# Pairing the k-v products of two attention units in one visit to the 64x64 tiling

## Chip, cores and metric

The kernel runs on one core of one Trainium2 chip. The metric is the device time of one execution in microseconds (us); lower is better. Single executions of the kernel before took 311.52, 308.06, 313.25 and 309.49 us, a median of 310.5.

## What is computed

Linear attention with softmaxes on q and k, followed by a two-layer block with ELU on all 4608 tokens:

```python
# q, k, v: (8 batches, 8 heads, 576 tokens, 64), float32
q_s = exp(q) / sum(exp(q), over the 64 features)
k_s = exp(k) / sum(exp(k), over the 576 tokens)
kv  = einsum('bhsd,bhse->bhde', k_s, v)
att = einsum('bhsd,bhde->bhse', q_s, kv)
x   = att.transpose(0, 2, 1, 3).reshape(4608, 512)
h   = x @ w_in                                     # (4608, 2048)
g   = where(h > 0, h, exp(min(h, 0)) - 1)
out = g @ w_out                                    # (4608, 512)
```

The maxima that the reference takes off before exp cancel, and the kernel leaves them out.

## The kernel before, in words

**Units.** The attention is cut into 16 units, two for each batch; a unit holds four heads: two on the partition halves f, two in the free dimension h. Its tokens are 9 chunks of 64. Tiles with a buffer number n % 2 are shared by every second unit; there is one raw v buffer `VR` for the units from 4 on, one transposed-q buffer `QT` and, from unit 4 on, one `qsT`.

**A unit's steps.** Loads of q, k and v, 576 KB each, from GpSimd's queue (L321 to L333). `stage1` (L359): exp of q and of k on ScalarE (L365, L368), a cast of v to bf16 `VB` on GpSimd (L373), and for q the sums, reciprocals and scaling on VectorE (L381, L385, L389). From unit 6 on, a DMA transpose of q from SP's queue (`turn`, L425) and a widening cast on GpSimd (`widen`, L433, L435). `kv_mm` (L451): 36 matmuls of 64x64 by 64x65 into columns 384 to 448 of the two banks of one PSUM tile (9 chunks, times 2 f, times 2 h); column 65 of v is ones and gives the sum over k. `m` (L466): a reciprocal and two multiplications on VectorE (L470, L474) make the block matrix `MBLK`. `ao_mm` (L483) in two parts of the chunks, x = 0 and 1 (`part`, L479): two full-array matmuls each, into the same PSUM tile `AB` (number 3), from where ScalarE copies them into the ring `XT` (L513).

**The ELU block.** `hg` (L534): eight 128x512 matmuls into PSUM tile 0 or 1 in turn (L545), exp on ScalarE (L554), then L571 and L573 on VectorE write `GT` (in the first two blocks every second group goes by L565 and L567). `out_mm` (L577, matmuls at L583) and `out_store` (L590, copy L600, stores L609) turn `GT` into output rows. There are nine blocks of 512 tokens with eight groups each.

**Order.** `Sched` is a list scheduler that plans every engine's order beforehand from fixed durations and a model of the loads; a load of a unit from 6 on is taken to land 5000 ns later than that model says (L331). Engines run their planned order in order, with semaphore waits. The main work is a list of `hg` groups; slot s is group s counted from block 0 (eight slots a block). Attention steps are hung on slots (L713 to L720), and an operation hung on a slot is not planned before the start of that slot's group. Unit n has a slot `begin` for stage1 and `use` for its output: units 4 to 7 have (8, 9), (10, 12), (12, 16), (14, 20), and from there (4n - 14, 4n - 8). `ao(n, 0)` stands at use + 1 and `ao(n, 1)` at use + 2; `ao(n, 1)` carries `kv_mm` of unit n + 1 in the same operation on TensorE, and with it the next k load, of unit n + 3, which overwrites the buffer that has just been read. So the k-v products of units 5 to 15 lie at slots 11, 14, 18, 22, 26 and so on to 50, one unit to a visit.

Of the kernel before, what the change touches and what calls it, by code (L numbers as in the profile page):

```python
# [3 lines left out]
AF = mybir.ActivationFunctionType  # L4
# [7 lines left out]
B, H, S, D = 8, 8, 576, 64  # L12
# [4 lines left out]
NU = 2 * B  # L17
CH = 9
BYDMA = 6
# [16 lines left out]
class Sched:  # L36
# [19 lines left out]

    def add(self, eng, dur, emit, key, R=(), W=(), X=(), dma=None, nbytes=0, after=(),
            follow=None, side=0):
        op = Op(eng, dur, emit, key, dma, nbytes)
        op.idx = len(self.ops)  # L60
        op.follow, op.side, op.late, op.gate = follow, side, False, self.gate
        for d in after:
            op.deps[d] = "raw"
        for res in list(R) + list(X):
            for d in self.w.get(res, ()):
                op.deps[d] = "raw"
        for res in list(W) + list(X):
            for d in self.r.get(res, ()):
                op.deps.setdefault(d, "war")
            for d in self.w.get(res, ()):  # L70
                op.deps.setdefault(d, "waw")
        op.deps.pop(op, None)
        for res in R:
            self.r.setdefault(res, []).append(op)
        for res in list(W) + list(X):
            self.w[res] = [op]
            self.r[res] = []
        self.ops.append(op)
        return op
# [164 lines left out]
def t_act(n, psum):  # L244
    return n / 1.2 + (90 if psum else 105)


def t_dve(n, fast=1):
    return n / 0.96 / fast + 75
# [6 lines left out]
class Gen:  # L256
# [49 lines left out]
    def init(self):  # L306
        S = self.S
        S.add("dve", 100, lambda e: e.memset(self.ID[:, :], 0.0), -95, W=["ID"])
        S.add("gp", 300, lambda e: e.affine_select(
            self.ID[:, :], self.ID[:, :], compare_op=ALU.not_equal, fill=1.0, base=0,  # L310
            pattern=[[-1, 128]], channel_multiplier=1), -38, X=["ID"])
        S.add("dve", 60, lambda e: e.memset(self.RZK[0][:, :], 0.0), -90, W=["RZK0"])
        S.add("act", 1400, lambda e: e.activation(self.RZK[0][:, :], self.RZK[0][:, :], AF.Exp), -80,
              X=["RZK0"])
        for i in range(2):
            S.add("dve", 150, lambda e, i=i: e.memset(self.VB[i][:, :, :, D:D + 1], 1.0), -8,
                  W=[f"VBone{i}"])
            S.add("dve", 300, lambda e, i=i: e.memset(self.MBLK[i][:, :, :].bitcast(F32), 0.0), -8,
# [37 lines left out]
        self.gpq = self.S.ops[-1]  # L356
        return self.gpq

    def stage1(self, n, key, vconv="gp"):  # L359
        S = self.S  # L360
        i = n % 2
        q, k, VB = self.RAW[i]["q"], self.RAW[i]["k"], self.VB[i]
        v, vname = self.raw("v", n)
        flat = lambda t: t[:, :, :, :].rearrange("p h c d -> p (h c d)")
        S.add("act", t_act(1152, False), lambda e: e.activation(flat(q), flat(q), AF.Exp),  # L365
              key - 3, X=[f"qR{i}"])
        ek = self.ek(i)
        S.add("act", t_act(1152, False), lambda e: e.activation(  # L368
            ek[:, :, :, :].rearrange("p h c d -> p (h c d)"), flat(k), AF.Exp),
            key - 2, X=[f"kR{i}"])  # L370
        hs = slice(0, 2) if vconv == "gp" else slice(0, 1)
        eng, t = ("gp", 1250) if vconv == "gp" else ("dve", t_dve(576) + 60)
        S.add(eng, t, lambda e: e.tensor_copy(  # L373
            VB[:, hs, :, 0:D], v[:, hs, :, :]), key - 50, R=[vname], W=[f"VB{i}"])
        self.conv = S.ops[-1]
        if vconv != "gp":
            S.add("act", t_act(576, False), lambda e: e.activation(
                VB[:, 1:2, :, 0:D], v[:, 1:2, :, :], AF.Copy), key - 50, R=[vname],
                W=[f"VB{i}x"])
            self.conv2 = S.ops[-1]  # L380
        S.add("dve", t_dve(1152) + 60, lambda e: e.tensor_reduce(  # L381
            self.ZQ[i][:, :, :].rearrange("p h c -> p (h c)"),
            q[:, :, :, :].rearrange("p h c d -> p (h c) d"), AX.X, ALU.add),
            key - 3, R=[f"qR{i}"], W=[f"ZQ{i}"])
        S.add("dve", 250, lambda e: e.reciprocal(self.RZQ[i][:, :, :], self.ZQ[i][:, :, :]),  # L385
              key - 3, R=[f"ZQ{i}"], W=[f"RZQ{i}"])
        rz = self.RZQ[i][:, :, :].unsqueeze(3).broadcast_to([128, 2, CH, D])
        qso = self.QS[self.alt(n)][:, :, :].rearrange("p c (h d) -> p h c d", h=2)
        S.add("dve", t_dve(1152) + 60, lambda e: e.tensor_tensor(  # L389
            qso, q[:, :, :, :], rz, ALU.mult),  # L390
            key - 3, R=[f"qR{i}", f"RZQ{i}"], W=[f"QS{self.alt(n)}"])
# [54 lines left out]
        self.S.add("pe", sum(p[0] for p in parts), mm, key, R=sum((p[1] for p in parts), []),  # L446
                   X=[f"b{2 * ps}", f"b{2 * ps + 1}"], side=1)

    KV = 384

    def kv_mm(self, n, ps):  # L451
        i = n % 2
        P, ek, VB = self.PS[ps], self.ek(i), self.VB[i]

        def mm(e):
            for c in range(CH):
                for f in range(2):
                    for h in range(2):
                        fs, hs = slice(f * 64, f * 64 + 64), slice(h * 64, h * 64 + 64)
                        x = f * 512 + self.KV  # L460
                        last = e.matmul(P[hs, x:x + D + 1], ek[fs, h, c, :],  # L461
                                        VB[fs, h, c, 0:D + 1], start=(c == 0), stop=(c == CH - 1))
            return last
        return CH * 45 + 100, [f"kR{i}", f"VB{i}", f"VB{i}x", f"VBone{i}"], mm

    def m(self, n, ps, key):  # L466
        S, i, rz = self.S, n % 2, self.RZK[n % 2]
        banks = [f"b{2 * ps}", f"b{2 * ps + 1}"]
        PV = self.PS[ps][:, :].rearrange("p (f x) -> p f x", f=2)[:, :, self.KV:self.KV + D + 1]
        S.add("dve", 180, lambda e: e.reciprocal(rz[:, :].unsqueeze(2), PV[:, :, D:D + 1]), key,  # L470
              W=[f"RZK{i}"], X=banks)
        for h in range(2):
            hs = slice(h * 64, h * 64 + 64)
            S.add("dve", 330, lambda e, h=h, hs=hs: e.tensor_tensor(  # L474
                self.MBLK[i][hs, :, h:128:2], PV[hs, :, 0:D],
                rz[hs, :].unsqueeze(2).broadcast_to([64, 2, D]), ALU.mult),
                key, R=[f"RZK{i}"], W=[f"MBLK{i}{h}"], X=banks)

    def part(self, n, x):  # L479
        cut = self.split(n // 2)  # L480
        return (0, cut) if x == 0 else (cut, CH)

    def ao_mm(self, n, x, ps):  # L483
        i = n % 2
# [129 lines left out]
    def program(self):  # L614
        S = self.S
# [10 lines left out]
        AB, C, D_ = 3, 2, 1  # L626
# [38 lines left out]
        def due(n):  # L665

            return when[n][1] + 4 if n in when else 3 + 4 * (n % 2)

        def kv(n):
            def go():  # L670
                self.side(AB, due(n), self.kv_mm(n, AB))
                self.m(n, AB, due(n) - 4)
            return n, go

        def ao(n, x, kvn=None):
            ps, eng = (C if x == 0 else AB, "both") if n == 3 else (AB, "act")

            def go():
                parts = [self.ao_mm(n, x, ps)] + ([self.kv_mm(kvn, ps)] if kvn else [])
                self.side(ps, due(n), *parts)  # L680
                self.xt(n, x, ps, due(n) - 4, eng)
                if kvn:
                    self.m(kvn, ps, due(kvn))
            return n, go

        def first(n):
            def go():
                self.stage1(n, due(n))
                if n >= BYDMA:
                    self.turn(n, due(n))  # L690
            return n, go

        def wide(n):
            if n < BYDMA:
                return n, lambda: self.tp(n, C if n == 3 else AB, due(n) - 4, ("act",))
            return n, lambda: self.widen(n, due(n))

        def loads(*tn):
            def go():
                for t, n in tn:  # L700
                    if n < NU:
                        self.load(n, t, due(n) - 20)
            return 0, go
# [6 lines left out]
        def at(s, *what):  # L710
            slots.setdefault(s, []).extend(what)

        for n in range(4, NU):  # L713
            begin, use = when[n]
            at(begin, first(n), loads(("v", n + 1), ("q", n + 2)))
            at(use - 2 if n >= BYDMA else use, wide(n))
            if n == 4:
                at(use, kv(n), loads(("k", n + 2)))
            at(use + 1, ao(n, 0))
            at(use + 2, ao(n, 1, n + 1 if n + 1 < NU else None), loads(("k", n + 3)))  # L720

        def piece(blocks):
            if steps:
# [9 lines left out]
        key = 0  # L733
# [82 lines left out]
```

## Time and profile before

| | before |
|---|---|
| runs shown | 308.06 to 313.25 us, median 310.5 |
| the profiled execution | 311.22 us, of which 309.4 are the span of the profile |
| PE busy | 296.3 us, 96% of the span, granted clock 0.994 on the mean |
| VectorE, ScalarE, GpSimd busy | 203.4, 162.0, 70.3 us |
| L583 and L545, 128x512 matmuls | 576 each, 144.9 and 144.0 us busy |
| L461, k-v matmuls | 576, 7.8 us busy by the modelled ends |
| L491, attention output matmuls | 64, 14.2 us busy |

A line of the profile's groups or timeline names the source line, engine, operation, the tiles written and read, and the count. Matmuls are pipelined and their ends are modelled; what TensorE really spends is read from the distance between starts. Brackets at the end of a timeline line give idle time ahead of it and what ended it. GpSimd is POOL, VectorE is DVE, ScalarE is ACT.

### The profile page before, as it was taken

To read this page: it belongs to the slowest core of one execution; us is meant where nothing else is said; L and a number is where in the kernel's file an instruction comes from. 1 tells how busy PE (TensorE), PEld (TensorE's weight loads), DVE (VectorE), ACT (ScalarE), POOL (GpSimd) and SP (SyncE) were. 2 spreads that over 40 slices of the span, in tenths; PEclk is the share of its full clock that TensorE was granted. 3 is DMA by queue.
4 is the path that set the end of the run, shared out by engine and by line. 5 is a ranking of instruction groups with operands and counts; after the bars stand their busy time and mean duration, and the time that the engine had idled before them with its cause. 6 is when DMAs were issued, how large, how long until landed. Compare 5 with 4: busy or idle time off the path is not lost.

```text
span 309.4 us, 4597 instructions
## 1 busy us (share of the span) xinstructions
PE 296.3 (96%) x1938; PEld 241.6 (78%) x1938; DVE 203.4 (66%) x244; ACT 162.0 (52%) x190; POOL 70.3 (23%) x84
## 2 busy tenths in 40 slices
PE   7789999989999979999999999999999999999994
PEld 7667787768788868888888888888888888888783
DVE  3837865798998969595969686875544445555500
ACT  4738757979666436464646373734343343333311
POOL 0790144341342435050414130301000000000000
PEclk9979999999999999999999999999999999999999
DMA  7999999797597783938382934131111121111122
GB/s 268 323 365 389 390 390 327 253 294 112 187 284 184 210 239 99 250 81 247 85 243 79 250 80 99 32 74 34 34 36 35 45 48 46 34 34 34 36 68 68
DMA packets 29589, 49.39 MB, mean 160 GB/s; under 512 B 13952, under 2 KB 13952, under 8 KB 29568
## 3 DMA queue, kind: packets, MB, share of 16 engines
q0 software_dynamic: 10336, 33.16, 35.2%
q1 hardware_dynamic: 19232, 15.93, 20.6%
q8 instruction: 15, 0.25, 0.3%
q14 instruction: 6, 0.05, 0.0%
HBM read 36.70 MB, written 9.44 MB: 149 GB/s over the span
## 4 chain that ended last, share of the span: by engine, by line
PE 86%; DVE 5%; DMA 4%; ACT 2%; issue 1%; POOL 1%; SPq 0%
PE PS L583 41%; PE PS L545 40%; DMA VR<-in_v_dram 2%; PE PS L491 2%; DMA W<-in_moe_w_in_dram 2%; DVE ESB L571 1%; PE PS L461 1%; DVE GT L573 1%; ACT ESB L554 1%; DVE QS L389 1%; DVE GT L567 1%; ACT ESB L565 1%; SPq L329 0%; DVE ZQ L381 0%; DVE MBLK L474 0%
## 5 line engine op out<-in xcount | busy, mean ns | idle before, releaser
L545 PE MATMUL PS<-XT,W 128*128 128x512 f32 x576 | 144.0, 394 | 2.8 <-DMA W<-in_moe_w_in_dram 1.2
L583 PE MATMUL PS<-W,GT 128*128 128x512 f32 x576 | 144.9, 393 | 1.7 <-DVE GT L573 1.7
L545 PEld LDWEIGHTS PS<-XT,W 128*128 128x128 f32 x576 | 108.3, 190 | 27.1 <-DVE GT L567 1.8
L583 PEld LDWEIGHTS PS<-W,GT 128*128 128x128 f32 x576 | 106.1, 188 | 24.2 <-DVE GT L573 2.6
L554 ACT ACTIVATE ESB<-PS 128x1024 f32<-128x1024 f32 x72 | 73.9, 1027 | 95.5 <-PE PS L545 95.3
L571 DVE TENSOR_SCALAR ESB<-ESB 128x1024 f32<-128x1024 f32 x64 | 55.5, 867 | 67.4 <-ACT ESB L554 67.1
L573 DVE TENSOR_TENSOR GT<-ESB,PS 128x1024 fp32r<-128x1024 f32 x64 | 78.2, 1221 | 2.2
L600 ACT ACTIVATE OSB<-PS 128x512 f32<-128x512 f32 x32 | 19.2, 600 | 37.0 <-PE PS L583 37.0
L381 DVE TENSOR_REDUCE ZQ<-QR 128x18 f32<-128x1152 f32 x16 | 21.6, 1349 | 6.2 <-ACT QR L365 6.1
L329 POOL DMA_DIRECT2D KR<-in_k_dram x14 | 10.2, 728 | 66.5 <-PE PS L461 66.5
L373 POOL CAST VB<-VR 128x1152 bf16<-128x1152 f32 x15 | 18.3, 1218 | 22.9 <-DMA VR<-in_v_dram 22.9
L389 DVE TENSOR_TENSOR QS<-QR,RZQ 128x1152 f16<-128x1152 f32 x16 | 22.1, 1382 | 0.6
L513 ACT ACTIVATE XT<-PS 128x640 fp32r<-128x640 f32 (+5 forms) x32 | 19.7, 618 | 3.1 <-PE PS L491 3.0
L435 POOL CAST qsT<-QT 128x1152 fp32r<-128x1152 f16 x10 | 13.7, 1372 | 31.0 <-PE PS L461 25.2
L365 ACT ACTIVATE QR<-QR 128x1152 f32<-128x1152 f32 x16 | 18.6, 1165 | 2.8 <-DMA QR<-in_q_dram 2.8
L368 ACT ACTIVATE KR<-KR 128x1152 bf16<-128x1152 f32 x16 | 18.6, 1160 | 1.2 <-DMA KR<-in_k_dram 1.2
L491 PE MATMUL PS<-qsT,MBLK 128*128 128x320 f32 (+3 forms) x64 | 14.2, 306 | 1.1 <-ACT XT L513 0.6
L491 PEld LDWEIGHTS PS<-qsT,MBLK 128*128 128x128 f32 x64 | 11.6, 189 | 4.5 <-DVE MBLK L474 1.0
L329 POOL DMA_DIRECT2D QR<-in_q_dram x14 | 10.3, 738 | 20.0 <-DVE QS L389 20.0
L567 DVE SCALAR_TENSOR_TENSOR GT<-PS,ESB 128x1024 fp32r<-128x1024 f32 x8 | 9.8, 1222 | 6.0 <-ACT ESB L565 6.0
L329 POOL DMA_DIRECT2D VR<-in_v_dram x14 | 10.4, 746 | 3.3 <-POOL VB L373 3.3
L474 DVE TENSOR_TENSOR MBLK<-PS,RZK 64x128 fp32r<-64x128 f32 x32 | 9.3, 289 | 1.1
(28 smaller groups left out, 76.0 us busy)
## 6 DMA issues: line engine op xcount, KB each, us to landing
out_dram<-OSB SPq DMA_DIRECT2D x64, 128.0 KB, 2.4
QR<-in_q_dram POOLq DMA_DIRECT2D x14, 576.0 KB, 5.8
KR<-in_k_dram POOLq DMA_DIRECT2D x14, 576.0 KB, 5.0
VR<-in_v_dram POOLq DMA_DIRECT2D x14, 576.0 KB, 6.4
W<-in_moe_w_in_dram POOLq DMA_DIRECT2D x8, 512.0 KB, 7.8
W<-in_moe_w_out_dram POOLq DMA_DIRECT2D x4, 1024.0 KB, 17.7
QR<-in_q_dram SPq DMA_DIRECT2D x2, 576.0 KB, 4.4
KR<-in_k_dram SPq DMA_DIRECT2D x2, 576.0 KB, 7.0
```

The source lines that it names most:

```text
L329: S.add(eng, ISSUE[eng], lambda e: e.dma_start(dst, src), key, W=[name], dma=f"{name}{eng}", nbytes=128 * 4608, follow=self.gpq if chain e ...
L365: S.add("act", t_act(1152, False), lambda e: e.activation(flat(q), flat(q), AF.Exp), key - 3, X=[f"qR{i}"])
L381: S.add("dve", t_dve(1152) + 60, lambda e: e.tensor_reduce(self.ZQ[i][:, :, :].rearrange("p h c -> p (h c)"), q[:, :, :, :].rearrange("p h ...
L389: S.add("dve", t_dve(1152) + 60, lambda e: e.tensor_tensor(qso, q[:, :, :, :], rz, ALU.mult), key - 3, R=[f"qR{i}", f"RZQ{i}"], W=[f"QS{se ...
L491: last = e.matmul(P[:, f * 512:f * 512 + n_], M[:, f, :], T[:, c0:c1, f * 64:f * 64 + 64], start=True, stop=True)
L513: S.add("act", t_act((h1 - h0) * n_, True), lambda e, dst=dst, src=src: e.activation(dst, src, AF.Copy), key, W=W, X=X)
L545: last = e.matmul(P[:, t * 512:(t + 1) * 512], self.W1[:, kc, tt * 128:(tt + 1) * 128], self.XT[:, kc, rc:rc + BLK], start=(kc == 0), stop ...
L554: S.add("act", t_act(1024, True), lambda e: e.activation(esb[:, :], P[:, :], AF.Exp), key, W=[f"E{i}"], X=banks)
L571: S.add("dve", t_dve(1024, 2) + 80, lambda e: e.tensor_scalar(esb[:, :], esb[:, :], 1.0, -1.0, ALU.min, ALU.add), key, X=[f"E{i}"])
L573: S.add("dve", t_dve(1024) + 90, lambda e: e.tensor_tensor(gt, esb[:, :], P[:, :], ALU.max), key, R=[f"E{i}"], W=gw, X=banks)
L583: last = e.matmul(dst, GT[:, jj, ts * 128:(ts + 1) * 128], self.W2[:, jj, :], start=(jj == 0), stop=(jj == 15))
L600: S.add("act", t_act(512, True), lambda e: e.activation(osb[:, :], src, AF.Copy), key, W=[f"O{i}0", f"O{i}1"], X=[f"b{bk}"])
```

## The change

The k-v products of units 6 and 7, 8 and 9, and so on to 14 and 15 are made in one operation on TensorE, one after the other. The column base moves from 384 to 382, so that two results of 65 columns end at column 512; the second stands at 447. Units 6 and 7 get an operation of their own at slot 16; the other pairs ride with `ao(n, 1)` of the odd unit n ahead of them, at slots 22, 30, 38 and 46. The `m` of both units follow one another.

The k part of `stage1` (exp of k and cast of v) of units 9, 11, 13 and 15 is split off and moves two slots forward, from `begin` of its unit to `begin` + 2 of the unit before; the next v load goes with it. The k loads follow the visits: units 8 and 9 at slot 16 (before: 14 and 18), 10 and 11 at 22 (before: 22 and 26), and so on. `part` now gives x = 1 the shorter part for batch 5 as well (units 10 and 11, cut 3), so that the columns of `ao(11, 1)` and two products fit in a bank. Units 0 to 5 keep their visits.

```diff
-    def stage1(self, n, key, vconv="gp"):
+    def stage1(self, n, key, vconv="gp", what="qk"):
...
+        if "q" in what:
+            S.add("act", t_act(1152, False), lambda e: e.activation(flat(q), flat(q), AF.Exp),
+                  key - 3, X=[f"qR{i}"])
+        if "k" in what:
...
+        if "q" not in what:
+            return
...
-    KV = 384
-
-    def kv_mm(self, n, ps):
+    KV = 382
+
+    def kv_mm(self, n, ps, at=KV):
...
-                        x = f * 512 + self.KV
+                        x = f * 512 + at
...
-        return (0, cut) if x == 0 else (cut, CH)
+        return (0, cut) if x == (cut < 5) else (cut, CH)
...
-                parts = [self.ao_mm(n, x, ps)] + ([self.kv_mm(kvn, ps)] if kvn else [])
+                cols = [(m, self.KV + (D + 1) * y) for y, m in enumerate(kvn)]
+                parts = [self.ao_mm(n, x, ps)] + [self.kv_mm(m, ps, y) for m, y in cols]
                 self.side(ps, due(n), *parts)
                 self.xt(n, x, ps, due(n) - 4, eng)
-                if kvn:
-                    self.m(kvn, ps, due(kvn))
+                for m, y in cols:
+                    self.m(m, ps, due(m), y)
...
+        def kv2(n):
+            def go():
+                cols = [(n, self.KV), (n + 1, self.KV + D + 1)]
+                self.side(AB, due(n), *[self.kv_mm(m, AB, y) for m, y in cols])
+                for m, y in cols:
+                    self.m(m, AB, due(m) - 4, y)
+            return n, go
...
-            at(begin, first(n), loads(("v", n + 1), ("q", n + 2)))
+            late = n > 7 and n % 2
+            at(begin, first(n, "q" if late else "qk"), loads(("q", n + 2)))
+            if not late:
+                at(begin, loads(("v", n + 1)))
+            if n > 6 and n % 2 == 0:
+                at(begin + 2, first(n + 1, "k"), loads(("v", n + 2)))
             at(use - 2 if n >= BYDMA else use, wide(n))
             if n == 4:
-                at(use, kv(n), loads(("k", n + 2)))
+                at(use, kv(n), loads(("k", 6)))
+            if n == 6:
+                at(use, kv2(n), loads(("k", 8), ("k", 9)))
+            pair = n > 6 and n % 2 and n + 1 < NU
             at(use + 1, ao(n, 0))
-            at(use + 2, ao(n, 1, n + 1 if n + 1 < NU else None), loads(("k", n + 3)))
+            at(use + 2, ao(n, 1, (n + 1, n + 2) if pair else (5,) if n == 4 else ()))
+            if n == 4:
+                at(use + 2, loads(("k", 7)))
+            if pair:
+                at(use + 2, loads(("k", n + 3), ("k", n + 4)))
```

More of the change, by code (lines that the diff above doesn't have):

```diff
@@ L364, in stage1 @@
         flat = lambda t: t[:, :, :, :].rearrange("p h c d -> p (h c d)")
[L365 to L380, printed above, removed]
+        if "q" in what:
+            S.add("act", t_act(1152, False), lambda e: e.activation(flat(q), flat(q), AF.Exp),
+                  key - 3, X=[f"qR{i}"])
+        if "k" in what:
+            ek = self.ek(i)
+            S.add("act", t_act(1152, False), lambda e: e.activation(
+                ek[:, :, :, :].rearrange("p h c d -> p (h c d)"), flat(k), AF.Exp),
+                key - 2, X=[f"kR{i}"])
+            hs = slice(0, 2) if vconv == "gp" else slice(0, 1)
+            eng, t = ("gp", 1250) if vconv == "gp" else ("dve", t_dve(576) + 60)
+            S.add(eng, t, lambda e: e.tensor_copy(
+                VB[:, hs, :, 0:D], v[:, hs, :, :]), key - 50, R=[vname], W=[f"VB{i}"])
+            self.conv = S.ops[-1]
+            if vconv != "gp":
+                S.add("act", t_act(576, False), lambda e: e.activation(
+                    VB[:, 1:2, :, 0:D], v[:, 1:2, :, :], AF.Copy), key - 50, R=[vname],
+                    W=[f"VB{i}x"])
+                self.conv2 = S.ops[-1]
+        if "q" not in what:
+            return
         S.add("dve", t_dve(1152) + 60, lambda e: e.tensor_reduce(
@@ L464, in kv_mm, with m @@
         return CH * 45 + 100, [f"kR{i}", f"VB{i}", f"VB{i}x", f"VBone{i}"], mm
-    def m(self, n, ps, key):
+    def m(self, n, ps, key, at=KV):
         S, i, rz = self.S, n % 2, self.RZK[n % 2]
         banks = [f"b{2 * ps}", f"b{2 * ps + 1}"]
-        PV = self.PS[ps][:, :].rearrange("p (f x) -> p f x", f=2)[:, :, self.KV:self.KV + D + 1]
+        PV = self.PS[ps][:, :].rearrange("p (f x) -> p f x", f=2)[:, :, at:at + D + 1]
         S.add("dve", 180, lambda e: e.reciprocal(rz[:, :].unsqueeze(2), PV[:, :, D:D + 1]), key,
@@ L673, in kv, with ao, first @@
             return n, go
-        def ao(n, x, kvn=None):
+        def ao(n, x, kvn=()):
             ps, eng = (C if x == 0 else AB, "both") if n == 3 else (AB, "act")
             def go():
-                parts = [self.ao_mm(n, x, ps)] + ([self.kv_mm(kvn, ps)] if kvn else [])
+                cols = [(m, self.KV + (D + 1) * y) for y, m in enumerate(kvn)]
+                parts = [self.ao_mm(n, x, ps)] + [self.kv_mm(m, ps, y) for m, y in cols]
                 self.side(ps, due(n), *parts)
                 self.xt(n, x, ps, due(n) - 4, eng)
-                if kvn:
-                    self.m(kvn, ps, due(kvn))
+                for m, y in cols:
+                    self.m(m, ps, due(m), y)
             return n, go
-        def first(n):
+        def kv2(n):
             def go():
-                self.stage1(n, due(n))
-                if n >= BYDMA:
+                cols = [(n, self.KV), (n + 1, self.KV + D + 1)]
[3 more added lines that the diff above has]
+            return n, go
+        def first(n, what="qk"):
+            def go():
+                self.stage1(n, due(n), what=what)
+                if n >= BYDMA and "q" in what:
                     self.turn(n, due(n))
```

## The prediction

> **What bounds the kernel now.** I read the shares of busy time, then the chain that ended last, then the windows by stage, then TensorE's own timeline around two slots that differ only in a k-v product. The first two say that TensorE sets the end.
>
> ```profile
> PE 296.3 (96%) x1938; PEld 241.6 (78%) x1938; DVE 203.4 (66%) x244; ACT 162.0 (52%) x190; POOL 70.3 (23%) x84
> ...
> PE 86%; DVE 5%; DMA 4%; ACT 2%; issue 1%; POOL 1%; SPq 0%
> ```
>
> The windows show where it does not: PE's busy time is below the length of the stretch from 60 to 112 us and full from 112 to 290. In the same early stretch DVE is busy for about nine tenths.
>
> ```profile
> 60.00:78.00 18.00, 16.61 (x147) 13.12 (x148) 16.35 (x24) 15.71 (x18) 6.53 (x8) 1.00 0.81 202
> 78.00:92.00 14.00, 13.70 (x95) 10.97 (x94) 12.92 (x15) 9.73 (x12) 5.88 (x7) 1.00 0.75 221
> 92.00:112.00 20.00, 18.35 (x116) 14.82 (x116) 18.00 (x20) 9.52 (x11) 8.89 (x10) 1.00 0.74 197
> ...
> 128.00:216.00 88.00, 88.00 (x597) 72.43 (x596) 66.03 (x76) 46.45 (x56) 20.97 (x20) 1.00 0.47 125
> ```
>
> So from 112 us on a nanosecond that leaves TensorE's queue leaves the time; ahead of that, orders matter as much as work. Third, TensorE alone, over a slot without a k-v product (unit 8's part 0) and one with (part 1 and unit 9's product):
>
> ```profile
> 114.47 0.46 PE L491 MATMUL PS<-qsT,MBLK 128*128 128x320 f32 x2
> 114.77 1.99 PE L583 MATMUL PS<-W,GT 128*128 128x512 f32 x8
> 116.60 1.98 PE L545 MATMUL PS<-XT,W 128*128 128x512 f32 x8
> 118.42 0.40 PE L491 MATMUL PS<-qsT,MBLK 128*128 128x256 f32 x2
> 118.75 0.49 PE L461 MATMUL PS<-VB,KR 64*64 64x65 bf16 x36
> 119.17 2.12 PE L583 MATMUL PS<-W,GT 128*128 128x512 f32 x8
> 121.12 0.40 PE L545 MATMUL PS<-XT,W 128*128 128x512 f32 x1
> ```
>
> Starts count: 116.60 - 114.47 = 2.13 us without, 121.12 - 118.42 = 2.70 with. The second has 2 x 64 columns less of attention output; eight 512-column matmuls take 116.60 to 118.42 = 1.82, so 128 columns are 0.06. One visit therefore costs 2.70 - 2.07 = **0.63 us**. Of that the 36 matmuls themselves are the smaller half: their row is 0.49 long, one of them 0.19 (their median), so 36 starts lie within 0.30. The other **0.33** is the visit: about 0.09 before the first start (0.33 from 118.42 to 118.75, against 0.24 for 512 columns at the full rate), 0.12 after the last (119.05 to 119.17), and 0.13 that the L583 group behind it takes longer (1.95 to the next start, against 1.82).
>
> **The change, part by part, against the profiled execution (span 309.4, time 311.22, 0.7 above the median of 310.5).**
>
> *Visits.* Units 6 to 15 have ten visits now and five afterwards; units 0 to 5 are untouched. The matmuls stay. Five times 0.33 is **-1.65**. Ends: if a second product costs its whole distance from first start to the next group (119.17 - 118.75 = 0.42), five times 0.21 is -1.05; if only the pace of the last starts counted (12 starts in 0.09, so 0.27 for 36) it is -1.8. I take 1.65, since the second product finds the array in its tiling already. The Trainium skill, page TensorEngine Tiling (Array Packing), section Instruction Overhead, speaks against this: about 60 cycles for each matmul, one column as slow as 60. At the pace of the L583 row (512 columns in 0.2275 us) 60 are 0.027, and 36 such 0.96 us as an estimate, more than a whole visit here: by it five pairings would cost 5 x (0.96 - 0.63) = +1.65. The row has 36 starts in 0.30 us, 8 ns each, and the row decides.
>
> *Own operation for units 6 and 7, part order of batch 5, columns 382 and 447.* The visit is counted above. The same matmuls and copies run in another order for units 10 and 11: zero, covered by the ring, whose chunks are due in slot 40 while the short part now comes in slot 38 (two slots of 3.6 us against one L513 copy of about 0.5). Odd columns are read by L470 and L474, 0.16 and 0.31 a piece, on an engine off the path: zero either way, with no row for it; even doubled, 0.77 a unit is under the DVE slack worked out below.
>
> *m of two units at once.* No instruction more, but 0.16 + 0.61 = 0.77 of DVE work of the odd unit comes four slots earlier, behind the even one's. Look at the DVE behind the visit at 118.75:
>
> ```profile
> 120.56 1.64 DVE L571 TENSOR_SCALAR ESB<-ESB 128x1024 f32<-128x1024 f32 x1
> 122.23 1.22 DVE L573 TENSOR_TENSOR GT<-ESB,PS 128x1024 fp32r<-128x1024 f32 x1
> 123.37 0.16 DVE L470 RECIPROCAL RZK<-PS 128x2 f32<-128x2 f32 x1
> 123.56 0.61 DVE L474 TENSOR_TENSOR MBLK<-PS,RZK 64x128 fp32r<-64x128 f32 x2
> ```
>
> L573 ends at 123.45 and frees the PSUM tile that the group at 124.76 writes: 1.31 of slack. 0.77 fits, and the alternate slots have no visit, so DVE gets back. Zero; at the other end, if the two k loads that now stand in POOL's queue ahead of the widening push L571 by another 0.72, 0.77 + 0.72 - 1.31 = 0.18 over, at four pairs +0.7.
>
> *POOL's queue.* The k loads (0.72 of issue each) go out in twos; casts and v loads of odd units from 9 on pass the widening of the even unit. POOL is busy 23% and its time is mostly waiting for k-v products; in the steady part a k load is issued some 13 us ahead of its exp (119.55 and 132.97), so that two at once still land in time. SP's queue (transposes, stores) keeps its order, zero. Where it can hurt is the stall that is there already:
>
> ```profile
> 102.02 3.40 DVE L571 TENSOR_SCALAR ESB<-ESB 128x1024 f32<-128x1024 f32 x1 [0.43 <-ACT ESB L554]
> ...
> 110.71 2.11 PE L583 MATMUL PS<-W,GT 128*128 128x512 f32 x8 [1.65 <-DVE GT L573]
> ```
>
> L571 usually takes 0.69. At 102.02 it waits out POOL's widening (102.62) and cast of v9 (103.71, ends 104.87), and ends 0.55 after the cast; DVE is late from there, and PE stands 1.65 at 110.71. The page SBUF — State Buffer, section Who interferes with whom, has the rule: one exclusive lock for VectorE's fast modes and GpSimd. By that rule a queued load's issue would hold it too, as a sentence by itself: two loads, 1.4. No row shows that: L571 at 108.72 took 0.69 beside the load issued at 109.09. Afterwards the cast of v9 stands before the visit, which takes 1.16 off that wait, and m of unit 9 puts 0.77 on. I take **0** net for the stall, ends -1.65 (gone) and +0.8.
>
> *New wait.* A visit now waits for exp of k and cast of v of both units, and `ao(7, 1)` waits with it; behind it on PE stand the groups. Cast v7 ended at 80.66 + 1.15 = 81.81, and PE could be at the slot 16 visit at 79.54: up to 2.4 with a hop. Cast v9 ended at 104.87, and PE was at `ao(7, 1)` at 100.77: up to 4.2. I take 0, since the planner puts the visit behind its own idea of these casts, and that adds 5 us to each load; TensorE then has other groups to run, and a later visit costs nothing until slot 25, where `ao(8, 0)` needs it.
>
> Sum: -1.65 + 0 + 0 = 309.6 for the profiled execution, and 310.5 - 1.65 = **308.9** as a median, its own range 308.7 to 310.2 by the ends of the visits and of DVE.
>
> **Rivals.**
> *The stall at 110.71 goes.* For: the cast that made it leaves its place. Against: two k loads and a second m take that place. 308.9 - 1.65 = 307.2.
> *PE waits for the younger unit's v* (the slower side). Place: visits 6/7 and 8/9; price 2.4 and 4.2 as above; it turns the gain into a loss from 1.65 of waiting on. For: v7 and v9 pass through one buffer, each load starting only after the cast before it (v9's load was issued at 93.50, landing about 6.4 later, cast 1.16: 101.1, just when PE is there). Against: the planner's 5 us. At 8/9 alone 308.9 + 4.2 = 313.1, at both 315.5.
> *No gain:* the 0.33 is a price of each product and not of the switch. For: nothing shows two products in a row before. Against: 36 starts in 0.30 us. 310.5.
>
> **How the numbers follow.** Forecast 0.53, stall gone 0.17, wait for v 0.22 (0.09 at one pair, 0.13 at both), no gain 0.08. About 1% (3.1 us) is what a measurement of this kernel can tell from no change. Faster by more: 0.12 of the second case, which lies right at that bound, and 0.03 of the first: 0.15. Slower by more: the wait at both pairs, 0.13. The rest, 0.72, is within. The range, 306.6 to 313.2, reaches from just under the stall's going to the wait at one pair; it leaves out the wait at both and a little below. I expect 308.9.
>
> **What would show it.** Eleven groups of starts at L461 in place of sixteen, five of them with 72 matmuls in about 0.6 us; each pair's slots 0.33 shorter in sum than before from 112 us on. A forecast gone wrong shows as idle PE ahead of L491 or L461 with POOL L373 as its end near 80 or 101 (wait for v), ahead of L583 or L545 with DVE L573 (stall kept or grown), or as a second product longer than 0.42.

## The result, and the profile after

The changed kernel takes 308.84 us as a median of 54 runs, against 310.18 of 78 runs of the kernel before: a ratio of 0.9961, 95% interval 0.9948 to 0.9975, or 0.8 to 1.6 us less. The profiled execution took 308.63 us, with a span of 306.8 (before: 311.22 and 309.4). Two further measurements gave 0.9943 (0.9917 to 0.9969) and 1.0008 (0.9972 to 1.0043): the second, alone, shows no difference. Medians are of all executions of a kernel, ratios of those within 1.5% of its fastest.

In the changed kernel the lines stand up to four further down: its L465, L495, L549, L587, L575 and L577 are L461, L491, L545, L583, L571 and L573 of the kernel before, and its L571 is L567. The page of the changed kernel: the same 1938 matmuls, and in the chain that ended last TensorE is still the largest share, though 72% instead of 86: the chain now runs back through a load of v that lands near 44 us, to the start-up.

```profile
PE 293.7 (96%) x1938; PEld 239.6 (78%) x1938; DVE 199.2 (65%) x244; ACT 162.4 (53%) x190; POOL 72.5 (24%) x84
...
PE 72%; DMA 10%; DVE 8%; POOL 5%; ACT 3%; issue 1%; SPq 0%; DVEq 0%
```

The same stretches in its windows (length, PE busy, PEld, DVE, ACT, POOL, granted clock, DMA share, GB/s): from 92 to 112 us PE is busy for 19.70 of 20 instead of 18.35, from 78 to 92 it has lost 0.45.

```profile
60.00:78.00 18.00, 16.60 (x115) 13.13 (x114) 16.01 (x20) 15.69 (x19) 5.83 (x8) 1.00 0.71 214
78.00:92.00 14.00, 13.25 (x127) 10.50 (x126) 12.65 (x17) 7.83 (x9) 6.62 (x8) 1.00 0.69 199
92.00:112.00 20.00, 19.70 (x158) 16.00 (x157) 15.18 (x19) 11.43 (x14) 8.82 (x9) 1.00 0.73 199
...
128.00:216.00 88.00, 87.92 (x600) 72.53 (x599) 63.64 (x77) 46.26 (x55) 20.68 (x20) 1.00 0.45 122
```

TensorE's timeline at the pair of units 10 and 11:

```profile
132.17 0.40 PE L495 MATMUL PS<-qsT,MBLK 128*128 128x256 f32 x2
132.50 0.78 PE L465 MATMUL PS<-VB,KR 64*64 64x65 bf16 x72
133.21 2.11 PE L587 MATMUL PS<-W,GT 128*128 128x512 f32 x8
135.15 1.98 PE L549 MATMUL PS<-XT,W 128*128 128x512 f32 x8
```

72 starts take 133.21 - 132.50 = 0.71 us to the next group, where 36 took 0.42: the second product costs 0.29. The edges are unchanged: 0.33 from L495 to the first product, and the group behind takes 1.94 instead of 1.82. And two places at which PE idles, with what ended it:

```profile
80.19 2.11 PE L549 MATMUL PS<-XT,W 128*128 128x512 f32 x8 [0.75 <-DVE GT L571]
...
109.33 2.12 PE L587 MATMUL PS<-W,GT 128*128 128x512 f32 x8 [0.30 <-DVE GT L577]
```

The first was 0.30 before, the second 1.65.

To add this up I take the distance from each matmul's start to the next, less its rate (227 ns for 512 columns), from the first matmul of slot 12 (65 us) to the last. "Edges" is what lies at the two ends of the visits and in the first matmul behind; "stalls" is every other excess of over 130 ns, without stretches of half clock. Start-up, which differs between executions, is outside.

| us | slot 12 to the last matmul | edges | stalls |
|---|---|---|---|
| before, two profiles | 239.44, 239.27 | 3.24, 3.24 | 2.27, 2.07 |
| changed, three profiles | 237.46, 237.40, 237.44 | 1.63, 1.63, 1.63 | 1.61, 1.60, 1.61 |

The visits take 1.61 us less. The stalls are another matter: before 0.46 at slot 17 and 1.82 (1.61) near 110; changed 0.91 at slot 17, 0.47 near 109 and 0.24 near 203. The rest, what the table leaves of the distance, is 0.2 to 0.3 more in the changed kernel, about as much as the smallest of these stalls; its cause is open.

### The profile page after: what moved, and what is told of

It is laid out like the page before. It is cut to its first block, busy times and chain, and to the rows that moved or that the text cites. A ratio compares the mean times of both kernels' runs of the same rounds, so it can differ in the third digit from the quotient of the medians.

```text
span 306.8 us, 4600 instructions
## 1 busy us (share of the span) xinstructions
PE 293.7 (96%) x1938; PEld 239.6 (78%) x1938; DVE 199.2 (65%) x244; ACT 162.4 (53%) x190; POOL 72.5 (24%) x84
## 4 chain that ended last, share of the span: by engine, by line
PE 72%; DMA 10%; DVE 8%; POOL 5%; ACT 3%; issue 1%; SPq 0%; DVEq 0%
PE PS L587 36%; PE PS L549 33%; DMA VR<-in_v_dram 10%; DVE GT L577 2%; PE PS L495 2%; POOL W L345 2%; DVE ESB L575 2%; DVE QS L393 1%; ACT ESB L558 1%; DVE ZQ L385 1%; POOL VB L375 1%; PE PS L465 1%; DVE GT L571 1%; POOL W L354 1%; ACT ESB L569 1%
## 5 line engine op out<-in xcount | busy, mean ns | idle before, releaser
L549 PE MATMUL PS<-XT,W 128*128 128x512 f32 x576 | 142.7, 392 | 3.4 <-DMA W<-in_moe_w_in_dram 1.4
L587 PE MATMUL PS<-W,GT 128*128 128x512 f32 x576 | 144.4, 392 | 0.4 <-DVE GT L577 0.3
L549 PEld LDWEIGHTS PS<-XT,W 128*128 128x128 f32 x576 | 106.9, 188 | 27.6 <-DVE GT L571 2.4
L587 PEld LDWEIGHTS PS<-W,GT 128*128 128x128 f32 x576 | 106.2, 188 | 22.9 <-DVE GT L577 1.8
L575 DVE TENSOR_SCALAR ESB<-ESB 128x1024 f32<-128x1024 f32 x64 | 49.6, 775 | 67.6 <-ACT ESB L558 67.2
L577 DVE TENSOR_TENSOR GT<-ESB,PS 128x1024 fp32r<-128x1024 f32 x64 | 78.2, 1221 | 2.2
L375 POOL CAST VB<-VR 128x1152 bf16<-128x1152 f32 x15 | 21.5, 1436 | 26.0 <-DMA VR<-in_v_dram 26.0
L439 POOL CAST qsT<-QT 128x1152 fp32r<-128x1152 f16 x10 | 12.4, 1243 | 56.0 <-PE PS L495 38.9
L393 DVE TENSOR_TENSOR QS<-QR,RZQ 128x1152 f16<-128x1152 f32 x16 | 23.4, 1464 | 0.5
L495 PE MATMUL PS<-qsT,MBLK 128*128 128x320 f32 (+3 forms) x64 | 14.2, 306 | 1.1 <-ACT XT L517 0.6
L495 PEld LDWEIGHTS PS<-qsT,MBLK 128*128 128x128 f32 x64 | 11.6, 189 | 4.5 <-ACT XT L517 1.0
L571 DVE SCALAR_TENSOR_TENSOR GT<-PS,ESB 128x1024 fp32r<-128x1024 f32 x8 | 9.8, 1224 | 6.4 <-ACT ESB L569 6.3
```

What stands on the lines that cost most here:

```text
L375: S.add(eng, t, lambda e: e.tensor_copy(VB[:, hs, :, 0:D], v[:, hs, :, :]), key - 50, R=[vname], W=[f"VB{i}"])
L393: S.add("dve", t_dve(1152) + 60, lambda e: e.tensor_tensor(qso, q[:, :, :, :], rz, ALU.mult), key - 3, R=[f"qR{i}", f"RZQ{i}"], W=[f"QS{se ...
L495: last = e.matmul(P[:, f * 512:f * 512 + n_], M[:, f, :], T[:, c0:c1, f * 64:f * 64 + 64], start=True, stop=True)
L549: last = e.matmul(P[:, t * 512:(t + 1) * 512], self.W1[:, kc, tt * 128:(tt + 1) * 128], self.XT[:, kc, rc:rc + BLK], start=(kc == 0), stop ...
L575: S.add("dve", t_dve(1024, 2) + 80, lambda e: e.tensor_scalar(esb[:, :], esb[:, :], 1.0, -1.0, ALU.min, ALU.add), key, X=[f"E{i}"])
L577: S.add("dve", t_dve(1024) + 90, lambda e: e.tensor_tensor(gt, esb[:, :], P[:, :], ALU.max), key, R=[f"E{i}"], W=gw, X=banks)
```

## The experiments

My theory was that each visit costs 0.32 us beside its matmuls and that this makes the gain. The rival was that the moved loads and casts make it, by way of the stall near 110. Each run has its ratio to the kernel before, with the interval.

**The changed kernel again.** 

> The changed kernel again, as the measure for the next ones on the same chip. Both theories expect about 1.2 to 1.8 us under the kernel before. What differs in the profile from the first one of the changed kernel shows which idle times of TensorE are fixed by the order and which come and go with the landing of loads.

Measured: 308.63, ratio 0.9943 (0.9917 to 0.9969). From slot 3 to the end no slot's first matmul differs from the first profile by more than 0.1 us once the start is aligned (-0.27 at slot 8, -0.31 at the end), so its three stalls belong to the order.

**Pairs split in two visits.**

```diff
-                parts = [self.ao_mm(n, x, ps)] + [self.kv_mm(m, ps, y) for m, y in cols]
+                kvs = [self.kv_mm(m, ps, y) for m, y in cols]
+                parts = kvs[:1] + [self.ao_mm(n, x, ps)] + kvs[1:] if len(kvs) > 1 else (
+                    [self.ao_mm(n, x, ps)] + kvs)
```

> The four pairs from unit 8 on keep their operation, slot and everything else, but the attention output's two matmuls stand between the two products, so that TensorE enters the 64x64 tiling twice. Theory (each visit costs about 0.32 us beside its matmuls): about 4 x 0.32 = 1.3 us slower than the changed kernel, that is near the kernel before, and from slot 27 on the distance to the changed kernel grows by about 0.3 at each of slots 30, 38 and 46. Rival (the gain is the stall near 110 us that got shorter when loads and casts moved): equal to the changed kernel within 0.3 us.

Measured: 309.19, ratio 0.9982 (0.9950 to 1.0014), on the chip on which the changed kernel had 0.9943. Its timeline has two visits around the output's matmuls:

```profile
133.37 0.48 PE L465 MATMUL PS<-VB,KR 64*64 64x65 bf16 x36
133.79 0.50 PE L495 MATMUL PS<-qsT,MBLK 128*128 128x256 f32 x2
134.22 0.48 PE L465 MATMUL PS<-VB,KR 64*64 64x65 bf16 x36
134.63 2.11 PE L587 MATMUL PS<-W,GT 128*128 128x512 f32 x8
```

Against the changed kernel slots 24, 31, 39 and 47 are each 0.30 to 0.32 later: the price, four times, 1.26 in the edges (2.89 against 1.63). But at slots 25 and 49 it takes 0.33 and 0.32 back: the waits for GT near 109 and 203 shrink, since TensorE comes to them later. Net 0.6 us by the profile. The medians are 0.56 apart (309.19 and 308.63), the ratios 0.0039, which is 1.2 us, and their intervals overlap. So the theory's price is right, the rival is wrong that nothing would change, and two of the four savings only lengthen a wait for VectorE.

The same run says how the gain is shared. From slot 12 on the split kernel needs 239.48 us, and 1.4 of that is a stretch of half clock at 65.6 us (last section) that the others don't have there. Without it, it is 1.2 to 1.3 us under the kernel before and 0.65 to 0.7 over the changed one. By the profiles, then, four pairs bring a third of the gain, and the new order around them, by way of the stall near 110, about two thirds. By the ratios (0.9982 and 0.9943) it is the other way round: two thirds for the pairs. The shares stay open between these two.

**The moves without the pairs.** From unit 9 on the k parts and v loads as in the changed kernel, every product alone:

```diff
...
-            if n == 6:
-                at(use, kv2(n), loads(("k", 8), ("k", 9)))
-            pair = n > 6 and n % 2 and n + 1 < NU
...
-            at(use + 2, ao(n, 1, (n + 1, n + 2) if pair else (5,) if n == 4 else ()))
-            if n == 4:
-                at(use + 2, loads(("k", 7)))
-            if pair:
-                at(use + 2, loads(("k", n + 3), ("k", n + 4)))
+            at(use + 2, ao(n, 1, (n + 1,) if n + 1 < NU else ()), loads(("k", n + 3)))
```

> Exp of k, cast of v and the next v load of units 9, 11, 13 and 15 two slots earlier and the part order of batch 5 as in the changed kernel, but every k-v product in a visit of its own, in the slots of the kernel before. Theory (the visits make the gain): within 0.5 us of the kernel before, apart from what the stall near 110 us does. Rival (the moved casts make it, by taking the 1.65 us stall away): 1.2 to 1.7 us under the kernel before, with no idle time of over 0.5 us ahead of L587 near 110 us.

Measured: 312.21, ratio 0.9991 (0.9945 to 1.0037); 241.14 us from slot 12 on, with edges of 3.28, stalls of 2.57 and 1.6 at half clock (last section). The stall near 110 is not gone but 2.1. VectorE and TensorE there:

```profile
101.58 3.37 DVE L575 TENSOR_SCALAR ESB<-ESB 128x1024 f32<-128x1024 f32 x1
...
110.53 3.17 PE L587 MATMUL PS<-W,GT 128*128 128x512 f32 x8 [1.95 <-DVE GT L577]
```

The planner left the cast of v9 behind the widening on GpSimd, and L575 waited out both, as before. In this execution, of 312.49 us, the earlier slots alone did not remove the stall, against the rival. The times don't settle it: three of the twelve took 307.8 to 308.0, the other nine 311.3 to 314.6, and none of the three was profiled. They may have been without the stall, and the interval reaches down to the rival's 1.2 to 1.7 us.

**Pairs from unit 8 on.** Units 6 and 7 as before, at slots 14 and 18:

```diff
-            if n == 6:
-                at(use, kv2(n), loads(("k", 8), ("k", 9)))
...
-            at(use + 2, ao(n, 1, (n + 1, n + 2) if pair else (5,) if n == 4 else ()))
-            if n == 4:
-                at(use + 2, loads(("k", 7)))
+            at(use + 2, ao(n, 1, (n + 1, n + 2) if pair else (n + 1,) if n < 7 else ()))
+            if n < 7:
+                at(use + 2, loads(("k", n + 3)))
```

> Units 6 and 7 keep single visits, at slots 14 and 18 with the k loads of the kernel before; pairs from unit 8 on. If a visit is worth its 0.32 us wherever it is, this is 0.3 us slower than the changed kernel. If the visit at slot 14 was hidden, because TensorE waits for VectorE's GT at slot 17 anyway (0.46 us there before, 0.91 in the changed kernel), then it is 0.3 us faster than the changed kernel, since only the visit of unit 7 is left in the full part, 0.62 instead of 0.91.

Measured: 309.39, ratio 0.9967 (0.9921 to 1.0013), but the profile needs 236.52 us from slot 12 on, 0.94 less than the changed kernel, with edges of 1.98 and stalls of 0.68. One more visit, 0.35 of edges, and ahead of slot 17:

```profile
81.52 0.72 PE L549 MATMUL PS<-XT,W 128*128 128x512 f32 x2 [0.30 <-DVE GT L571]
```

0.30 as in the kernel before, not 0.75. The visit of unit 6 at slot 14 was hidden: taken out, TensorE comes to the same wait 0.45 earlier, and the product is paid at slot 18, where nothing hides it. The stall near 109 is absent in this profile too (0.47 in the changed kernel), and counts for as much. The times don't confirm the better order, so I ran it once more.

> Pairs from unit 8 on, once more, beside the changed kernel on the same chip. Its first profile had 0.94 us less TensorE time from slot 12 on than the changed kernel, yet its times were spread from 307.1 to 312.4. If the order is better as such, its median is 0.5 to 1 us under the changed kernel. If the spread belongs to the order (an idle time that comes in some executions only), about two in five of its times are over 311 us again and the median is not under the changed kernel's.

Measured: 308.17, ratio 0.9953 (0.9917 to 0.9988), 1.1 us under the changed kernel beside it (309.3). But its profile needs 238.55 us from slot 12 on, two more than its first: L393, which overwrites the tile that the transpose of q reads, waited 2.9 us for that transfer, and VectorE's delay reached TensorE ahead of L587 (1.22) and, at 115.59, ahead of the output's matmuls (0.47).

```profile
106.11 1.36 DVE L393 TENSOR_TENSOR QS<-QR,RZQ 128x1152 f16<-128x1152 f32 x1 [2.91 <-DMA QT<-QS]
...
108.10 1.22 DVE L577 TENSOR_TENSOR GT<-ESB,PS 128x1024 fp32r<-128x1024 f32 x1
109.24 3.46 DVE L575 TENSOR_SCALAR ESB<-ESB 128x1024 f32<-128x1024 f32 x1
...
109.38 2.11 PE L587 MATMUL PS<-W,GT 128*128 128x512 f32 x8 [1.22 <-DVE GT L577]
```

The order can win 0.9 and doesn't always. As a faster version it stays unclear: 0.8 us over the changed kernel on one chip, 1.1 under it on the other.

> The changed kernel, beside the other two of this call: 308.2 to 309, 1.2 to 1.8 us under the kernel before, idle times ahead of slot 17 and near 109 and 203 us as in both of its profiles (0.9, 0.5, 0.2).

Measured: 309.3, ratio 1.0008 (0.9972 to 1.0043); stalls of 0.91, 0.47 and 0.24 again. On this chip the changed kernel was not the faster one, though its profile is the same to 0.06 us.

**Eight visits at each pair, and the same work in one.** Full-array matmuls of 32 columns, spread or in front; every round starts its own sum (`True` is `False` in the second kernel):

```diff
...
+            for _ in range(1 if True else 8):
+                other()
...
+                    if True and left[0] and k and k % 2 == 0:
+                        other()
```

> The changed kernel, with eight full-array matmuls of 32 columns added at each of the five pairs: one ahead of the products, seven spread between their rounds, so that TensorE enters the 64x64 tiling eight times at each pair instead of once. To allow that, every round writes over the one before: the sum over the chunks is left out, in this kernel and in the next alike; order and work of the other engines are those of the changed kernel. Theory (0.32 us for each entry and exit, beside the matmuls): 35 more visits than the next kernel, so 35 x 0.32 = 11 us slower than it, less some 1 us of waits that the longer visits take the place of. The part of the 0.32 that lies in the following 512-column group (0.1) may shrink with 32 columns behind it: no less than 35 x 0.2 = 7 us. Rival (a price of the product, not of the entry): within 1 us of the next kernel.

> The same 72 product matmuls and eight matmuls of 32 columns at each pair as in the kernel before this one, with all eight ahead of the products: one visit at each pair. Both theories: 40 small matmuls are 40 x 0.02 to 0.06 = 0.8 to 2.4 us more TensorE time than the changed kernel.

Measured: 316.1 and 309.37, ratios 1.0196 (1.0156 to 1.0237) and 0.9980 (0.9948 to 1.0012): 6.7 us between them. Edges 9.47 and 1.59, so 7.88 for 35 visits, 0.225 each. That still holds the small matmul between two visits, which takes 0.03 where eight stand in a row; the whole distance from slot 12 on grew by 7.04 (238.00 to 245.04), 0.20 each. The second kernel needs 0.5 more than the changed one, with stalls that are 0.45 shorter (1.16), so 1.0 for its small matmuls. At one pair of the first kernel:

```profile
107.73 0.19 PE L817 MATMUL PS<-ID 128*128 128x32 f16 x1
107.85 0.26 PE L833 MATMUL PS<-VB,KR 64*64 64x65 bf16 x8
108.03 0.19 PE L817 MATMUL PS<-ID 128*128 128x32 f16 x1
108.15 0.26 PE L833 MATMUL PS<-VB,KR 64*64 64x65 bf16 x8
```

From product to product 0.30 us, of which two rounds are 0.065 by the 0.29 for nine. In and out is a price of the visit and not of the product. It is the lower end that I gave, 0.2: what is missing against 0.32 is about the 0.1 in the following 512-column group, which has no place behind 32 columns.

**The stall near 110 by itself.** In the kernel before, the widening of unit 8 is planned a slot later:

```diff
-            at(use - 2 if n >= BYDMA else use, wide(n))
+            at(use - 1 if n == 8 else use - 2 if n >= BYDMA else use, wide(n))
```

> The kernel before, single visits, with one step moved: the widening cast of unit 8 on GpSimd one slot later, so that it no longer stands between the k load at 101.9 and the cast of v9. Theory on the stall: TensorE's 1.65 us near 110 come from L571 waiting out widening and cast on GpSimd (3.40 instead of 0.69); with one of the two gone L571 ends 1.16 earlier and the stall is 0.5 or less, as in the changed kernel: 1.2 us under the kernel before, about equal to the changed one, with all sixteen visits. Rival (the visits make the whole difference between the kernels): equal to the kernel before within 0.4 us.

Measured: 310.8, ratio 1.0009 (0.9983 to 1.0035), with a profile at a clock of 0.85 throughout, which can't be laid beside the others.

> The kernel before with the widening cast of unit 8 one slot later, again, because its first profile ran at a clock of 0.85 throughout and can't be laid beside the others. Theory on the stall: L571 near 102 us takes 2.3 instead of 3.4, and TensorE's idle time near 110 is 0.5 to 0.7 instead of 1.65. Rival (the stall has another cause, the backlog on VectorE as a whole): over 1.2 as before.

Measured: 310.56, ratio 1.0032 (0.9999 to 1.0065). In the profile:

```profile
101.34 2.31 DVE L571 TENSOR_SCALAR ESB<-ESB 128x1024 f32<-128x1024 f32 x1 [0.43 <-ACT ESB L554]
```

2.31 as worked out, TensorE idles 0.6 ahead of L583, the stall is 0.72 instead of 1.82, and 238.40 us are needed from slot 12 on, 1.0 less than before. So GpSimd's chain made that stall in that execution. The times do not show the 1.0. The reason may be that the kernel before has this stall in other forms:

> The kernel before, profiled a second time. Its times lie in two groups, 308.0 to 309 and 310 to 312. If the stall near 110 us is fixed by the order, this profile has it again: L571 of 3.4 us near 102 and 1.6 to 2 us of idle time ahead of L583, and the groups come from elsewhere (the clock, the start). If the stall comes and goes with who is first at GpSimd's and VectorE's contested step, a profile of the lower group has L571 at 0.7 to 2.3 and less than 0.8 of idle time, with the rest of the order unchanged.

Measured: 309.74, ratio 0.9988 (0.9939 to 1.0037). The second profile of the kernel before has a stall of 1.61, with L571 at 0.69:

```profile
100.86 0.69 DVE L571 TENSOR_SCALAR ESB<-ESB 128x1024 f32<-128x1024 f32 x1 [0.43 <-ACT ESB L554]
...
105.11 1.36 DVE L389 TENSOR_TENSOR QS<-QR,RZQ 128x1152 f16<-128x1152 f32 x1 [1.58 <-DMA QT<-QS]
106.38 1.64 DVE L571 TENSOR_SCALAR ESB<-ESB 128x1024 f32<-128x1024 f32 x1
```

Neither outcome that I had written down: the stall is there, with another cause, the transpose of q, for which L389 waited. What is the same is the place: VectorE comes late out of 100 to 110 us, and the output's matmuls at slot 25 start only when it has written the GT group just ahead of them (L573 until 110.65 and L583 at 110.71 in the first profile).

**m first.** Pairs from 8, with `self.m(m, ps, due(m) - 8, y)`; the `m` of the single units 5 to 7 go ahead with it.

> Pairs from unit 8 on, as tried before, and the three VectorE steps of a pair's units with a key 8 smaller, so that the planner takes them ahead of the ELU steps. It is meant as a faster version: the idle time ahead of L587 near 203 us (0.22) came where both units' steps stood ahead of L575. Expected 0.9 us less TensorE time from slot 12 on than the changed kernel, as pairs from 8 gave, and 0.2 for the stall near 203; against it, that they now delay an earlier L575 by up to 1.5 us, which the 1.3 us of slack there need not cover: then a stall of up to 0.3 at each of the four pairs.

Measured: 309.83, ratio 0.9999 (0.9976 to 1.0021). The stall near 203 is gone, but two new ones of 1.05 came, at the pairs at 131 and 163 us, and 238.59 us are needed from slot 12 on, 1.1 more than in the changed kernel; VectorE and TensorE at the first:

```profile
134.69 2.52 DVE L575 TENSOR_SCALAR ESB<-ESB 128x1024 f32<-128x1024 f32 x1
...
138.53 0.73 PE L549 MATMUL PS<-XT,W 128*128 128x512 f32 x2 [0.90 <-DVE GT L577]
```

Both units' steps ahead of L575 take 1.66 (133.00 to 134.66), and push it under GpSimd's widening and cast. That is more than the 1.3 us of slack.

## Why the prediction held, and where its steps were off

*Visits, -1.65.* Right as the price: -1.61 in the edges, 0.29 for the second product where I had 0.30, 0.20 to 0.225 a visit without the following group, 0.32 with it. The eleven groups of starts, five of them with 72 matmuls, came as forecast.

*All five counted.* This step failed. I had read that TensorE waits before 112 us, and still priced the pair of units 6 and 7 like the rest. Its saving at slot 14 went into the wait at slot 17 (0.46 to 0.91). Units 6 and 7 in single visits gave that back, at 0.35 of edges. Nor does every nanosecond count from 112 us on, as I had it: by the split pairs, the savings at units 8 and 9 and at 14 and 15 went into the waits near 109 and 203 us (0.33 and 0.32). Of the five savings two reached the end in these profiles.

*m of two units, 0 with an end of +0.7.* 0.24 near 203, at one pair of four; splitting the pairs took it away, and so did the m steps at other times. Where they went ahead of L575, the slack of 1.3 that I had worked out was the limit, as the two stalls of 1.05 show.

*The stall near 110, 0 with ends of -1.65 and +0.8.* Mis-sized: 1.82 and 1.61 in the two profiles of before, 0.47 in all three of the changed kernel, so -1.1 to -1.4. I had expected two k loads to take the place of the cast. But L575 at 107.33 started with the first load's issue and took 0.69, and the second m came behind the ELU step.

```profile
107.33 1.55 POOL L329 DMA_DIRECT2D KR<-in_k_dram  x2 [8.59 <-PE PS L465]
107.33 0.69 DVE L575 TENSOR_SCALAR ESB<-ESB 128x1024 f32<-128x1024 f32 x1
```

*Wait for v, the slower rival.* It did not come: in the changed kernel's waits TensorE stands 0.7 us in all for L375's VB at L465, near 11 and 46 us, both ahead of the first pair. The five pairs did not wait for v.

*The sum.* By the first profiles -1.61 - 1.35 + 0.45 + 0.24 = -2.3, and -2.0 with the small rest; by the ratio -1.2. That the point forecast of -1.65 stood between these is luck: terms that I had set to nothing have opposite signs, and the largest of them, the stall, outweighs what the pairs bring net by the profiles. What makes the times gain less than the profiles is open. Single times of the kernel before reach down to 307.87, near the fastest of the changed one beside it, 307.73, so the stall near 110 may be absent in some of its executions; neither of its two profiles shows that. The half clock of the last section may have a part. The profiled executions of the changed kernel had a mean granted clock of 0.998 or 0.999. Its 17 executions at 0.996 or more have a median of 308.20, against 310.20 for 20 such executions of the kernel before in the later measurements: 2.0, as in the profiles. At 0.990 to 0.995 it is 309.07 (33) against 310.07 (72), 1.0. The 20 reach from 307.8 to 311.8 and come from three chips, so this is a hint and not shown.

## What to carry to other kernels

A change of tiling is paid per visit, so products that need it belong together; the price is read from the distance between starts across a visit and across its neighbour without one. A saving is worth its size only where the engine that saves has nothing to wait for behind it: look for the next wait on that engine, and count the saving only as far as that wait doesn't take it. Where the order comes from a planner, moving one step changes which operations meet on other engines, and such meetings can outweigh the step itself.

## What the runs showed of the hardware

TensorE's clock was halved for one stretch of 3.4 us after idle time. In the profile of the moves without the pairs, TensorE idled 1.95 us ahead of 110.53; the windows (PEclk is the third number from the right) then show 0.50:

```profile
107.00:111.20 4.20, 2.25 (x11) 1.55 (x10) 4.13 (x5) 1.02 (x1) 1.99 (x3) 1.00 0.70 190
111.30:114.70 3.40, 3.40 (x9) 2.67 (x8) 1.27 (x2) 0.60 (x1) 0.50 (x1) 0.50 0.88 279
114.70:118.00 3.30, 3.30 (x16) 2.73 (x15) 0.82 (x2) 1.91 (x3) 0.00 (x0) 1.00 0.46 137
```

Nine matmuls started in 3.4 us where 15 have room at 227 ns: 1.6 us lost behind a stall of 2.1. The kernel before idled 1.65 at the same place and lost nothing there; its own half-speed stretch lay at 16.7 to 20.1 us. The splitting of the pairs had one at 65.6, behind idle times of 0.55 and 0.85. So a stall can cost nearly twice its length in one execution and not in the next. One stretch of 3.4 us at half speed takes 0.0055 off the mean clock of a 307 us span, so the mean tells how many an execution had: of the 54 executions of the changed kernel, 17 at 0.997 or more have a median of 308.20 us, 33 at 0.992 to 0.994 one of 309.07, four at 0.983 one of 313.07.

VectorE's L575 against GpSimd: started at 107.33, with a load's issue, it took 0.69. Started within one (109.24, with a load's issue until 109.91), it waited for that, for the widening and for the cast (end 112.15) and took 3.46. The Trainium skill, page SBUF — State Buffer, section Who interferes with whom, says that of VectorE in a two-port mode and GpSimd the one that issues first has the shared ports for its whole instruction. Both rows agree with that. Close behind a load's start it came out both ways. In the first profile of the kernel before, L571 started 0.12 us behind one and took 3.40; in the second it started 0.13 behind and took 0.69, and there the load's issue took longer, 0.96 instead of 0.72:

```profile
101.90 0.72 POOL L329 DMA_DIRECT2D KR<-in_k_dram  x1 [5.80 <-PE PS L461]
...
100.73 0.96 POOL L329 DMA_DIRECT2D KR<-in_k_dram  x1 [6.28 <-PE PS L461]
```

The prediction said that no row shows a load's issue holding L571. The row at 102.02 does: it started 0.60 ahead of the widening, so the load held it until then.
